# Batch 1's product of q and k-transposed-v in float32, with a newly derived list of steps

## The chip, the cores and the metric

The kernel runs on one core of a Trainium2 chip. The metric is device time in microseconds (us). PE is TensorE, DVE is VectorE, ACT is ScalarE, POOL is GpSimd, and SP is SyncE, whose queue issues all transfers of this kernel. Between the engines only semaphores order the work; within one engine instructions run in the order of the program.

## The reference

Batch 8, 8 heads, 576 tokens, 64 channels a head; all in float32.

```python
q_s = softmax(q, axis=-1)            # over a head's 64 channels
k_s = softmax(k, axis=2)             # over the 576 tokens
kv  = einsum('bhsd,bhse->bhde', k_s, v)
x   = einsum('bhsd,bhde->bhse', q_s, kv)      # heads side by side: (8, 576, 512)
gate_pre = sum over t of conv_w[t] * x shifted down by 4 - t tokens   # 5 taps, zeros ahead
gate = sigmoid(gate_pre)
val  = x @ w_val                     # 512 x 512
out  = (gate * val) @ w_out          # 512 x 512
```

## The kernel before

The eight batches run through one pipeline. For each batch b, kv is summed from k and v by head pairs, q is transposed (q_turn, then q_turned copies it out of PSUM), and `attend b p` makes block p (128 of the 512 channels, all 576 tokens) of x in PSUM. From there x_high and x_low split a block into two float32r parts, first and four taps make the gate (a tap is one DVE instruction, or a scaled copy on ACT and an addition on POOL), sigmoid closes it. `value b m` multiplies x by w_val in three float32r products (low weights by high x, high by high, high by low), gated multiplies val by the gate, g_high and g_low split the result, `project b n` multiplies by w_out in the same way, and store copies a block out and sends it to memory. Weights arrive as 64-bit words (load_words) and are turned to float32 and split by part, field, scaled, signed, joined, w_high and w_low in the first 60 us. k's maximum over the tokens comes for batches 0 and 1 from a copy laid out by channels (load_kc, k_top, k_raise, k_turn), for the others from blocks km (load_km, k_peak), which go by way of memory (k_row, k_spread) to all partitions (k_sub, k_exp).

`attend` has two forms. For a batch in F32_BATCHES, batch 0 alone before, the main 512 tokens are one float32 product of kvd and the transposed q (`qh`). For the others kv is split by kv_high and kv_low and q by the type of qT and q_low, and three float32r products are summed: low kv by high q, high by high, high by low. The last 64 tokens are a float32 product in both.

The order is a list written out by hand or program, ORDER, of some 900 steps in one sequence; each step issues its instructions on its engines, so each engine and SP's queue run their share of it in that order. A letter behind a step names the engine: a ACT, v DVE, p POOL; l and r are the left and right half of the tokens. `warm n` issues n transposes into a spare bank; `warm 0` issues none. PSUM has two banks for x, q's transposes and the like (tag "x") and two for products (tag "mm"). The words, kvs and qTlo tiles share four buffers; the parts f of the weights and the km blocks share three; q, k and v have two buffers each. A load whose buffer is in use stops SP's queue, and all loads and stores behind it.

## Time and profile before

| | |
|---|---|
| median of three runs | 322.0 us (321.49 to 322.12) |
| the profiled execution | 320.3 us, its span 318.5 us |
| busy: PE | 297.3 us (93%) |
| busy: DVE | 271.5 us (85%) |
| busy: ACT | 204.6 us (64%) |
| busy: POOL | 188.7 us (59%) |
| read from memory, written | 41.4 MB, 9.5 MB |

PE's ends are modelled and its instructions overlap, so a pace is read from the distance of starts, not from durations. The page's busy shares are means over stages; the chain of waits and the timeline show what a stage waits for. A duration on DVE or ACT has some 0.06 us of overlap with the next one's start.

### The profile page before, as it was taken

Reading aid. Unit: us, or ns where it says so; the run is one execution under the profiler, and the core shown is the slowest. Engines: PE = TensorE matmul, PEld = TensorE weight load, DVE = VectorE, ACT = ScalarE, POOL = GpSimd, SP = SyncE. Lnnn points to the kernel's source line nnn. Section 1 sums busy time; section 2 is a strip of 40 time slices with the busy share of each in tenths; the row PEclk is TensorE's granted clock in tenths of the full one; section 3 lists DMA queues with packets and bytes.
Section 4 is the critical chain, followed back from the end, with each engine's and each line's share of the span. In section 5 each row is a group of like instructions: output and inputs, shape, how many; then the busy total and the mean of one; then the engine's idle time right before and its main releaser. Section 6 shows DMA issues by size and latency. Waiting matters only on the chain.

```text
span 318.5 us, 6426 instructions
## 1 busy us (share of the span) xinstructions
PE 297.3 (93%) x2557; PEld 276.4 (87%) x2557; DVE 271.5 (85%) x374; ACT 204.6 (64%) x316; POOL 188.7 (59%) x157
## 2 busy tenths in 40 slices
...
GB/s 250 370 390 174 410 396 199 194 8 175 238 264 264 74 181 139 254 189 112 143 64 313 50 232 283 160 16 355 82 0 37 39 77 2 0 74 76 0 42 108
DMA packets 20525, 51.25 MB, mean 161 GB/s; under 512 B 2832, under 2 KB 7312, under 8 KB 17808
## 3 DMA queue, kind: packets, MB, share of 16 engines
...
q8 instruction: 20, 0.33, 0.4%
...
HBM read 41.39 MB, written 9.45 MB: 160 GB/s over the span
## 4 chain that ended last, share of the span: by engine, by line
PE 55%; DVE 19%; DMA 16%; issue 4%; ACT 4%; SPq 1%; DVEq 0%; ACTq 0%
PE out L542 22%; PE val L542 20%; DVE gate L524 5%; DMA km<-in_k_strided 5%; PE x L498 4%; PE kv L433 4%; DMA words<-in_w_out 3%; DMA out<-o 2%; DMA q<-in_q 2%; DMA q<-in_q_tail 2%; PE qTps L465 2%; DVE qm L347 2%; DVE g L563 2%; DVE qs L362 2%; DVE kpk L274 2%
## 5 line engine op out<-in xcount | busy, mean ns | idle before, releaser
L524 DVE SCALAR_TENSOR_TENSOR gate<-x,cw,gate 128x575 f32<-128x575 f32 (+3 forms) x99 | 78.0, 807 | 3.3 <-POOL gate L528 1.5
L528 POOL TENSOR_TENSOR gate<-gate,far 128x572 f32<-128x572 f32 (+3 forms) x29 | 39.5, 1363 | 39.2 <-ACT far L527 38.9
L542 PE MATMUL out<-gh,w_out_lo 128*128 128x288 f32 x256 | 57.0, 301 | 0.7 <-ACT gh L160 0.7
L542 PE MATMUL val<-xh,w_val_lo 128*128 128x288 f32 x256 | 56.5, 302 | 0.8 <-DVE o L162 0.7
L542 PE MATMUL out<-gl,w_out_hi 128*128 128x288 f32 x256 | 55.6, 296 | 0.9 <-DVE gl L571 0.9
L542 PE MATMUL val<-xl,w_val_hi 128*128 128x288 f32 x256 | 55.0, 296 | 0.9 <-DVE xl L518 0.9
L542 PE MATMUL out<-gh,w_out_hi 128*128 128x288 f32 x256 | 55.4, 295 | 0.0
L542 PE MATMUL val<-xh,w_val_hi 128*128 128x288 f32 x256 | 54.8, 295 | 0.0
L571 POOL TENSOR_TENSOR gl<-g,gh 128x576 fp32r<-128x576 f32 x25 | 36.8, 1476 | 29.5 <-ACT gh L160 23.1
L542 PEld LDWEIGHTS out<-gl,w_out_hi 128*128 128x128 f32 x256 | 41.4, 188 | 1.4 <-DVE gl L571 1.4
L542 PEld LDWEIGHTS val<-xh,w_val_lo 128*128 128x128 f32 x256 | 40.9, 188 | 1.8 <-DVE o L162 0.9
L542 PEld LDWEIGHTS val<-xl,w_val_hi 128*128 128x128 f32 x256 | 41.2, 188 | 1.2 <-DVE xl L518 1.2
L542 PEld LDWEIGHTS out<-gh,w_out_lo 128*128 128x128 f32 x256 | 41.2, 189 | 1.0 <-ACT gh L160 1.0
L542 PEld LDWEIGHTS out<-gh,w_out_hi 128*128 128x128 f32 x256 | 41.5, 188 | 0.0
L542 PEld LDWEIGHTS val<-xh,w_val_hi 128*128 128x128 f32 x256 | 41.3, 188 | 0.0
L389 POOL TENSOR_TENSOR q<-q,qs 128x512 f32<-128x512 f32 x25 | 26.2, 1070 | 14.7 <-DVE qs L364 14.7
L563 DVE TENSOR_TENSOR g<-val,gate 128x576 f32<-128x576 f32 x32 | 23.9, 749 | 9.9 <-PE val L542 7.3
L527 ACT ACTIVATE far<-x,cw 128x572 f32<-128x572 f32 (+3 forms) x29 | 21.0, 737 | 14.2 <-DVE gate L524 9.3
L160 ACT CAST gh<-g 128x576 fp32r<-128x576 f32 x25 | 16.7, 672 | 17.5 <-DVE g L563 17.4
L160 ACT COPY o<-out 128x576 f32<-128x576 f32 (+1 forms) x22 | 13.5, 618 | 22.1 <-PE out L542 12.1
L531 ACT ACTIVATE gate<-gate 128x576 f32<-128x576 f32 x32 | 21.6, 685 | 6.1 <-DVE gate L524 3.5
L289 POOL TENSOR_TENSOR k<-k,kmax 128x512 f32<-128x512 f32 x18 | 24.9, 1397 | 0.9 <-DMA kmax<-krow 0.9
...
## 6 DMA issues: line engine op xcount, KB each, us to landing
out<-o SPq DMA_DIRECT2D x31, 288.0 KB, 2.3
v<-in_v SPq DMA_DIRECT2D x8, 1040.0 KB, 7.7
...
km<-in_k_strided SPq DMA_DIRECT2D x24, 288.0 KB, 3.2
...
kc<-in_k_channels SPq DMA_DIRECT2D x8, 288.0 KB, 8.1
...
```

The costliest lines, as they stand in the source:

```text
L160: nc.scalar.copy(out=out, in_=in_)
L289: engine(e).tensor_sub(kk[r, cs], kk[r, cs], mx[r, cs])
L389: engine(e).tensor_mul(qq, qq, s.unsqueeze(2).broadcast_to([P, H, D]))
L433: nc.tensor.matmul(acc[h * D:(h + 1) * D, p, :], T["k", b][:, c, cs] if c < 4 else ktz[b % 2][:, cs], T["v", b][:, c, hd] if c < 4 else T[ ...
L498: nc.tensor.matmul(ps[:, :MAIN], a, z, start=(i == 0), stop=(i == len(parts) - 1))
L524: nc.vector.scalar_tensor_tensor(out=a, in0=x, scalar=w, in1=a, op0=ALU.mult, op1=ALU.add)
L527: nc.scalar.activation(part, x, AF.Copy, scale=w)
L528: nc.gpsimd.tensor_add(a, a, part)
L531: nc.scalar.activation(T["gate", b, p], T["gate", b, p], AF.Sigmoid)
L542: nc.tensor.matmul(ps[:, cs], a[:, kb, ms], z[kb][:, cs], start=(kb == 0 and i == 0), stop=(kb == NB - 1 and i == 2),)
L563: nc.vector.tensor_mul(T["g", b, m], T["val", b, m], T["gate", b, m])
L571: engine(e).tensor_sub(T["gl", b, m], T["g", b, m], T["gh", b, m].bitcast(F32))
```

## The change

Batch 1 joins F32_BATCHES: its four x products are single float32 products, its qT is float32, and the steps kv_high 1, kv_low 1, q_low 1 0 and q_low 1 1 leave the list. The list is written anew: 902 steps in place of 906, nearly all of them moved against others, one of the two `warm 8` gone. No function is changed. Over the list 15 taps move from DVE to ACT and POOL, 12 g_low from POOL to DVE, three stores from DVE to ACT, three q_sub from DVE to POOL, two q_mul from DVE to ACT. The loads have another order; near the start q's first piece leads, k 2 stands where q 2 stood, and q 2 and k 3 come later. The last product is project 7 0 whole; before it was the left half of project 7 3.

```diff
-F32_BATCHES = (0,)
+F32_BATCHES = (0, 1)
...
-    load_kc 0 1, load_q 0 0 2, load_words 8, k_top 0 1, load_ident, q_lift 0 0, q_max 0 0 2, q_peak 0 0 2,
-    load_kc 0 0, k_top 0 0, load_words 1, load_kc 0 3, load_q 0 2 5, field 1, q_top 0 0 2 v, field 8, load_words 3,
...
-    k_top 0 2, load_kc 1 2, k_top 1 1, load_v 0, load_kc 1 3, w_high 1 a, load_kc 1 0, scaled 3 v, q_peak 0 2 5,
...
-    q_mul 0 2 v, kv 0, scaled 0 a, q_mul 0 1 p, q_mul 0 3 p, k_top 1 0, warm 8, q_turn 0 0, field 2, kv_norm 0 v,
...
-    q_mul 0 4 p, joined 0 p, part 2 a, tail_turn 0, load_q 2, tail_turned 0 a, load_k 3, signed 2, attend 0 1,
...
-    sigmoid 0 3, q_low 1 0, attend 1 0, q_turned 1 1 a, g_high 0 2 a, q_sub 2 0 p, g_high 0 1 a, load_kt 2, q_low 1 1,
...
-    load_km 3 3, attend 1 2, k_sub 2 3 p, first 1 2 a, k_sub 2 4 p, project 0 3, store 0 2 a, k_sub 2 1 p,
...
-    g_high 7 3 v, g_low 7 3 v, g_low 7 2 p, project 7 2, project 7 1, store 7 2 v, store 7 1 a, project 7 3 r,
-    project 7 0, store 7 3 a r, store 7 0 v, project 7 3 l, store 7 3 a l,
+    load_q 0 0 2, load_words 8, load_ident, q_max 0 0 2, field 8, q_lift 0 0, part 8 a, load_kc 0 1, load_kc 0 0,
+    load_words 1, q_peak 0 0 2, load_kc 0 3, load_q 0 2 5, q_top 0 0 2 a, k_top 0 1, load_words 3, load_kc 1 2,
...
+    joined 3 p, q_sum 0, k_tail_turn 0, q_exps 1 0 p, q_exps 1 3 p, k_top 1 0, k_top 1 3, k_turn 0 1, load_v 0,
+    k_top 1 1, k_tail_turned 0 a, q_exps 1 2 p, q_mul 0 2 v, q_mul 0 3 p, q_mul 0 1 p, joined 8 p, q_mul 0 4 v,
+    k_turned 0 1 a, scaled 0 a, k_raise 1 3, q_mul 0 0 a, kv 0, q_turn 0 0, w_high 3 a, tail_turn 0, k_raise 1 0,
+    signed 0, load_words 2, field 2, q_turned 0 0 a, kv_norm 0 v, k_raise 1 1, joined 0 p, q_turn 0 1,
+    tail_turned 0 a, scaled 2 p, q_sum 1, attend 0 1, load_words 5, field 5, load_words 4, part 2 v, load_k 2,
+    signed 2, load_v 1, q_turned 0 1 a, first 0 1 a, load_words 7, x_high 0 1 a, tap 0 1 3 v, w_low 3 p, w_high 0 a,
...
+    first 0 2 a, load_q 2, kv_norm 1 a, tap 0 3 2 v, load_k 3, x_low 0 3, load_kt 2, part 5 a, value 0 0, tap 0 2 3 v,
...
+    x_high 1 3 v, x_high 1 2 a, x_low 1 2, sigmoid 1 0, x_low 1 3, tap 1 2 3 v, value 1 0, first 1 3 v, tap 1 3 3 v,
+    warm 0, k_sub 2 1 p, load_km 4 1, load_q 3, q_exp 2, project 0 3, tap 1 2 2 v, warm 0, gated 1 0, tap 1 3 2 a,
...
+    load_km 5 2, first 2 0 a, x_high 2 1 a, store 1 0 a, k_sub 3 4 p, x_low 2 0, tap 2 0 3 v, load_k 4, k_sub 3 3 p,
...
+    g_high 7 2 a, value 7 3, gated 7 3, g_low 7 2 p, g_high 7 3 a, g_low 7 3 v, project 7 1, project 7 3 l,
+    store 7 1 a, project 7 3 r, project 7 2, store 7 3 a l, store 7 2 v, store 7 3 a r, project 7 0, store 7 0 a,
```

## Rows read from the trace of the kernel before

**Rows 1.** The chain of waits from 286 us on: start, length (us), work.

```profile
302.52 12.80 PE out L542 x96
```

**Rows 2.** PE's timeline: start, length (us), line, work, shape, count.

```profile
45.55 0.52 PE L542 MATMUL val<-xh,w_val_lo 128*128 128x288 f32 x2
87.69 0.51 PE L433 MATMUL kv<-v,k 128*64 128x65 f32 x10
```

**Rows 3.** PE's timeline: in brackets the idle time before, and its releaser.

```profile
82.31 0.54 PE L542 MATMUL val<-xl,w_val_hi 128*128 128x288 f32 x2 [0.93 <-DVE xl L518]
```

**Rows 4.** PE's groups from 87.7 us: busy us, mean ns, idle before.

```profile
L498 PE MATMUL x<-qT,kvs 128*128 128x512 f32 x48 | 16.1, 417 | 2.4 <-DVE qTlo L475 1.1 <-ACT far L527 1.1
L433 PE MATMUL kv<-v,k 128*64 128x65 f32 x384 | 14.6, 223 | 0.4 <-DVE o L162 0.4
```

**Rows 5.** PE's timeline around two kinds of x product.

```profile
32.74 1.08 PE L498 MATMUL x<-qT,kvd 128*128 128x512 f32 x2
33.65 0.33 PE L499 MATMUL x<-qTt,kvd 128*128 128x64 f32 x2
74.05 0.63 PE L498 MATMUL x<-qT,kvs 128*128 128x512 f32 x2
74.75 0.33 PE L499 MATMUL x<-qTt,kvd 128*128 128x64 f32 x2
```

**Rows 6.** Groups by line and form: busy us, mean ns, idle before.

```profile
L475 DVE TENSOR_TENSOR qTlo<-qTps,qT 128x1024 fp32r<-128x1024 f32 x14 | 16.7, 1214 | 0.5 <-ACT qT L160 0.5
L524 DVE SCALAR_TENSOR_TENSOR gate<-x,cw,gate 128x573 f32<-128x573 f32 x27 | 21.7, 808 | 1.8 <-POOL gate L528 1.4
L528 POOL TENSOR_TENSOR gate<-gate,far 128x572 f32<-128x572 f32 x11 | 15.9, 1447 | 5.3 <-ACT far L527 5.1
L160 ACT COPY o<-out 128x576 f32<-128x576 f32 x20 | 12.7, 639 | 16.8 <-issue 9.0 <-PE out L542 6.8 <-DMA out<-o 0.9
```

**Rows 7.** DVE's timeline: q's reduction, then three x_low.

```profile
11.96 1.75 DVE L347 TENSOR_REDUCE qm<-q 128x24 f32<-128x1536 f32 x1 [0.16 <-DMA q<-in_q_tail]
47.74 0.75 DVE L518 TENSOR_TENSOR xl<-x,xh 128x576 fp32r<-128x576 f32 x1
81.51 1.41 DVE L518 TENSOR_TENSOR xl<-x,xh 128x576 fp32r<-128x576 f32 x2
```

**Rows 8.** ACT's timeline: q_raise 0 2 and the first gate of batch 0.

```profile
20.90 0.60 ACT L420 ACTIVATE q<-qlps 128x512 f32<-128x512 f32 x1 [0.31 <-PE qlps L416]
33.00 0.72 ACT L512 ACTIVATE gate<-x,cw 128x576 f32<-128x576 f32 x1
```

**Rows 9.** Sums of waits: us in total, times, longest; SP's queue, then DVE.

```profile
SPq L196 <- PE qTtps L481: 9.2, 1, 9.2
DVE kpk L274 <- DMA km<-in_k_strided: 4.1, 4, 1.8
```

**Rows 10.** Instructions on gl: duration ns least/median/most.

```profile
L571 POOL TENSOR_TENSOR gl<-g,gh x25: 1422/1430/1938, 55.8 to 301.0; 128x576 fp32r<-128x576 f32 x25
L571 DVE TENSOR_TENSOR gl<-g,gh x7: 745/757/1683, 61.1 to 304.0; 128x576 fp32r<-128x576 f32 x7
```

**Rows 11.** Issues of transfers: count, KB each, median us to landing.

```profile
v<-in_v SPq DMA_DIRECT2D x8, 1040.0 KB, 7.7
out<-o SPq DMA_DIRECT2D x31, 288.0 KB, 2.3
out<-o SPq DMA_DIRECT2D x2, 144.0 KB, 1.7
```

**Rows 12.** ACT's timeline at the end.

```profile
315.34 0.40 ACT L160 COPY o<-out 128x288 f32<-128x288 f32 x1 [4.35 <-PE out L542]
```

**Rows 13.** One stretch: busy us by engine, granted clock, DMA share, GB/s.

```profile
13.00:14.00 1.00, 0.77 (x4) 0.34 (x4) 1.00 (x3) 0.74 (x2) 0.27 (x2) 0.50 1.13 459
```

**Rows 14.** PE's timeline: k_turn 0 0 and k_turn 0 1.

```profile
11.84 1.79 PE L319 MATMUL kps<-ident,kc 128*128 128x128 f32 x8
21.26 1.04 PE L319 MATMUL kps<-ident,kc 128*128 128x128 f32 x8
```

More of the change, by code (lines that the diff above doesn't have):

```diff
@@ L43 @@
-    q_turn 0 1, load_words 4, field 4, q_turned 0 0 a, signed 0, q_turned 0 1 a, scaled 2 a, q_sum 1, w_high 3 v,
-    q_mul 0 4 p, joined 0 p, part 2 a, tail_turn 0, load_q 2, tail_turned 0 a, load_k 3, signed 2, attend 0 1,
-    k_raise 1 2, first 0 1 a, x_high 0 1 a, load_v 1, field 5, tap 0 1 3 v, tap 0 1 2 v, tap 0 1 1 v, k_raise 1 0,
-    joined 2 p, k_raise 1 3, attend 0 0, k_tail_turn 1, w_low 3 p, warm 8, first 0 0 a, x_low 0 1, x_high 0 0 a,
-    tap 0 1 0 v, k_turn 1 0, w_high 0 a, k_tail_turned 1 a, tap 0 0 3 v, q_mul 1 3 p, x_low 0 0, scaled 5 a,
@@ L68 @@
-    g_high 1 1 a, tap 1 3 0 v, g_low 1 1 v, sigmoid 1 2, value 1 2, gated 1 2, load_km 4 0, warm 0, tail_turn 2,
-    kv_high 2 a, q_turn 2 0, k_sub 3 0 v, k_peak 4 0, tail_turned 2 a, sigmoid 1 3, q_turn 2 1, load_v 3,
-    q_turned 2 0 a, g_low 1 0 p, g_high 1 2 a, q_turned 2 1 a, q_low 2 0, k_sub 3 4 p, load_q 3, kv_low 2 p,
-    g_low 1 2 p, value 1 3, attend 2 1, q_low 2 1, attend 2 0, x_high 2 1 a, gated 1 3, q_max 3, first 2 1 a,
-    g_high 1 3 a, first 2 0 a, k_sub 3 1 p, load_km 4 2, tap 2 0 3 v, x_low 2 1, tap 2 0 2 v, g_low 1 3 p,
@@ L93 @@
-    q_turn 4 0, k_sub 5 3 p, tap 3 3 0 v, q_sub 5 2 p, q_turn 4 1, kv_norm 4 v, kv_high 4 v, value 3 2,
-    q_turned 4 0 a, tail_turned 4 a, kv_low 4 p, value 3 3, q_sub 5 3 p, q_turned 4 1 a, g_low 3 0 p, k_peak 6 1,
-    sigmoid 3 3, q_low 4 0, gated 3 2, q_low 4 1, attend 4 0, gated 3 3, first 4 0 a, attend 4 1, load_km 7 3,
-    g_high 3 2 v, load_q 6, x_high 4 0 a, g_high 3 3 v, g_low 3 2 p, first 4 1 v, q_exp 5, load_k 6, g_low 3 3 p,
-    tap 4 1 3 a, tap 4 0 3 v, x_low 4 0, project 3 2, tap 4 1 2 a, tap 4 0 2 v, x_high 4 1 a, project 3 1,
```

168 lines of the change are left out of this document (88 added, 80 removed).

## Prediction

> **What bounds the kernel now.** The page's busy shares come first: PE is the busiest engine and DVE the second, and neither share says which of them sets the end. So I went on to the chain of waits and to PE's timeline. From 286 us the chain is PE alone: the last four out products take 12.80 us, 3.20 us a product [rows 1]. Before the first val product at 45.55 us PE runs in pieces: nearly each step there waits for a transfer, DVE or ACT. Between 45.55 and the third kv product at 87.69 us [rows 2] it stops for DVE's results, longest for the low part of an x block, 0.93 us [rows 3]. After 87.69 us it idles 2.4 us ahead of the x products and 0.4 us ahead of kv, and hardly anywhere else [rows 4]. So three stages have three limits: DVE (with ACT and DMA) up to 46 us, DVE against PE up to 88 us, PE after that. Each is costed by itself.
>
> **Part 1: batch 1's x products (attend 1).** An x product in three float32r parts goes from 74.05 to 74.75 us in its main piece, 0.70 us; one in float32 from 32.74 to 33.65 us, 0.91 us [rows 5]. Four of them: 4 x 0.21 = +0.84 us of PE work. Removed are two q_low on DVE, 1.21 us each [rows 6], so 2.42 us, and kv_high on ACT and kv_low on POOL, for which nobody waited. Where the two q_low stood, 58 to 63 us, DVE works without a pause, and PE waits for DVE afterwards [rows 3]; so DVE's 2.42 us count, and PE's 0.84 us are covered as long as PE still waits there for more than that. Were DVE no limit, the part would cost 0.84 us.
> The Trainium skill (FP8 and Floating Point Precision, TensorE Precision Notes) counts four passes for true float32, against three single passes here: by it the ratio would be 4/3, an estimate of 0.93 us from 0.70, and the sum would be 0.1 us larger; the row is used.
>
> **Part 2: the list up to the first val product.** New and old load the same bytes ahead of q's second piece (kc 0 1, 0 0 and 0 3, q's first piece, words 8 and 1, ident), so DVE's reduction of that piece, which starts at 11.96 us when q's tail has landed [rows 7], is taken as unmoved. From its end to the last x_low of batch 0 DVE had 39 steps, 35.2 us by the mean durations of their groups, and took 34.8 us (13.71 to 48.49 us, first and last of them in [rows 7]): no gaps. The new list has 38 steps, 34.3 us there: four taps, scaled 3 and w_high 3 go, two other taps, q_mul 0 4, part 2 and field 7 come. That is -0.9 us. Against it stands ACT. From the end of q_raise 0 2 (21.50 us) to the first gate of batch 0 (33.00 us) [rows 8] ACT had 13.0 us of steps in 11.5 us, since instructions overlap at their ends; the new list puts k_raise 1 3, 1 0, 1 1 and w_high 3 ahead of that gate, 14.3 us, so 12.7 us at the same overlap. q_raise 0 2 itself ends some 0.9 us sooner, since the new list has less PE work before it, so the gate comes at 33.3 us in place of 33.0. Walking DVE on from there by hand (each step after the last, each tap after its gate), x_low 0 3 ends at 48.3 us against 48.49. I take 0; the bounds are -0.9 us (DVE's sum alone) and +3 us (ACT's steps without overlap, and half the clock, rival A). SP's queue improves: SP stood 9.2 us at load_q 2, with all later loads behind it [rows 9]; in the new list k 2 and v 1 go there, whose buffers are free, and q 2 stands behind v 2 and km 2 1.
>
> **Part 3: from the first val product to kv 2.** From x_low 0 3 to x_low 1 3 DVE had 38 steps and 32.3 us, and took 34.4 us (48.49 to 82.92, [rows 7]): 2.1 us of pauses, mostly for km transfers, for which DVE waits 4.1 us in all [rows 9]. The new list has 36 steps and 29.9 us: 2.42 us less for q_low, the rest exchanges. The km loads are queued earlier, so I keep 0.6 us of the pauses: x_low 1 3 ends at 48.3 + 29.9 + 0.6 = 78.8 us. value 1 0 can end 0.7 us later. New is that project 0 3 (3.2 us) follows it in place of leading it; then comes value 1 1 (3.2 us): kv 2 starts at 78.8 + 0.7 + 6.4 = 85.9 us in place of 87.69. That is -1.7 us, with PE's 0.84 us of part 1 inside. Bounds: -0.3 (all pauses stay) and -2.4 us (none). ACT's work from x_low 0 3 to the last q_turned of batch 2 grows from 37.1 to 39.8 us in some 47 us, so it has room, though not much.
>
> **Part 4: from kv 2 to the last val products.** Fifteen more taps go from DVE (0.81 us each) to ACT with an addition on POOL (1.45 us) [rows 6], and twelve g_low go from POOL (1.43 us) to DVE (0.76 us at the median) [rows 10]. Over the whole list DVE has 13.8 us less, ACT 18 us more (two more table loads among it), POOL 10 us more. PE's steps are the same but for their order, so only PE's 2.8 us of idle [rows 4] can be regained, or new idle be made. DVE's results for batch 2's val products come 4.7 us of its work earlier. I take -1.0 us, with bounds -2.8 and +3: load_v 3 now stands behind k 4 and a store, about 10.6 us of PE work before kv 3, and v's landing takes 7.7 us [rows 11] without a megabyte of k ahead of it.
> What speaks against the change in this part: DVE's seven g_low lasted 745 ns at least, 757 at the median and 1683 at most [rows 10], so one at least was held. The Trainium skill (SBUF — State Buffer, Who interferes with whom) says that a DVE instruction with two SBUF inputs and a GpSimd one that reads SBUF contend, and that the one that comes second waits for the other to end; the row agrees with it in some of the seven, and by that rule at its worst the time is that of rival B.
>
> **Part 5: the end.** The old list ends with half an out product: a copy of 0.40 us and a transfer of 144 KB, 1.7 us [rows 11, 12]. The new list ends with a whole tile: 0.64 us for ACT's copy [rows 6] and 288 KB, 2.3 us [rows 11]. +0.24 + 0.6 = +0.84 us; nothing covers it, and this is the surest term.
>
> **Sum.** 0 - 1.7 - 1.0 + 0.8 = -1.9 us. The profiled execution took 320.3 us, its span 318.5 us; so 318.4 us for one like it. The median of the three runs is 322.0 us, 1.7 us above; taken from that, 320.1 us.
>
> **Rivals.**
> A, no change: the gain is lost at the start. In the new list kv 0 waits for v 0, which is loaded behind three kc, and for k_tail_turned, by ACT's walk until 24.8 us. PE's step before it ends at about 21.1 us, so PE would stand 3.6 us, and the eight warming transposes behind kv 0 are gone. After the pauses around 9 us PE's granted clock was 0.50 (1.2 GHz) at 13 us [rows 13], and k_turn 0 0 took 1.79 us where k_turn 0 1 took 1.04 at 2.4 GHz [rows 14]. At half the clock kv 0 and the turns cost some 2 us more on the way to batch 0's first x, and value 0 0 is 1.9 us late: 322.0 us. For it: ACT and PE have no slack between 21 and 33 us. Against it: DVE has other work to do until 35 us.
> B, slower: DVE and POOL hold each other. Nineteen g_low on DVE, more additions on POOL: if each of the twelve moved took 1.68 us in place of 0.76, DVE gets 11 us back of its 13.8. Then parts 3 and 4 regain nothing, part 1's 0.84 us and part 5's 0.84 us stand, and one more wait of the size of 0.93 us [rows 3] comes in the middle: 322.0 + 0.8 + 0.8 + 0.9 = 324.5 us. It decides once the mean g_low on DVE passes about 1.3 us. Against it: the median of the row.
> C, faster still: DVE's relief removes all of PE's 2.8 us after kv 2, and the start gains its 0.9 us: 322.0 - 0.9 - 2.4 - 2.8 + 0.8 = 316.7 us.
> That the change doesn't do what it says: batch 1's x products would still read a qTlo at 60 us, with DVE's 2.4 us, and the time would be 322 us. I give it next to nothing, since the tuple F32_BATCHES alone decides it.
>
> **Chances.** The forecast, 318.4 to 321.3 us, 0.45; C and what lies toward it 0.15; A, 321.4 to 322.6 us, 0.17; B and any other slower case 0.23. A difference under 0.2% (0.64 us) can't be told from no change here. Faster 0.60, same 0.17, slower 0.23. The range takes in C to the edge and B with some 0.7 us of a late v 3: 316.5 to 325.2 us.
>
> **What would show it.** Part 1: four x products of batch 1 at 0.91 us in the main piece, and no qTlo before batch 2. Part 2: value 0 0 starts between 45 and 46.5 us; at 47.5 or later it is A, and PE's clock between 22 and 30 us tells which half of it. Part 3: kv 2 at about 86 us. Part 4: PE's idle after kv 2 below 2.8 us; kv 3 waiting for v would be the load order, long g_low on DVE would be B. Part 5: 0.84 us more from the last product to the end. The prediction is wrong if PE idles more than before in the middle, which sums per engine can't exclude: they say that no engine is full, not that no step comes late.

## The result and the profile after

The changed kernel takes 323.7 us (median of 20 executions, 321.2 to 326.2) against 321.5 us for the kernel before (20 executions, 318.3 to 326.5): 1.0092 times as long, 95% interval 1.0065 to 1.0119. The ratio, here and in the table below, leaves out executions more than 1.5% above the fastest of their kernel (three of the 20 here, three of e15's 12, two of e17's 6); the two medians, which leave out none, differ by 0.7%. The changed kernel is slower by 0.9%. The forecast was 320.1 us and faster.

The profiled execution of the changed kernel took 324.0 us, its span 322.1 us, 3.6 us more than before. Line numbers are one lower than in the kernel before. First the page: PE's busy time with its share and count, the granted clock in 40 slices, and the group of the taps on DVE (busy us, mean ns, idle before).

```profile
PE 299.2 (93%) x2545; PEld 278.7 (87%) x2545; DVE 265.9 (83%) x358; ACT 222.4 (69%) x350; POOL 198.9 (62%) x166
...
PEclk9797999989999999999979999999999999999999
...
L523 DVE SCALAR_TENSOR_TENSOR gate<-x,cw,gate 128x575 f32<-128x575 f32 (+3 forms) x84 | 66.9, 807 | 0.8
```

DVE was busy 265.9 us in place of 271.5. The forecast sum of moved steps was 13.8 us less; so some 8 us came back, as longer instructions; the places that matter are shown below. ACT has 222.4 us (18 more, as summed) and POOL 198.9 us (10 more, as summed). In the row of the clock the 7s and the 8 (at 8, 24, 64 and 161 us) are slices that hold a stretch at half speed.

PE's timeline (start, length in us, line, work, shapes, count, and in brackets the idle time before with its releaser) shows the places that matter, in order of time:

```profile
45.63 0.53 PE L541 MATMUL val<-xh,w_val_lo 128*128 128x288 f32 x2
...
61.31 1.08 PE L497 MATMUL x<-qT,kvd 128*128 128x512 f32 x2
62.22 0.33 PE L498 MATMUL x<-qTt,kvd 128*128 128x64 f32 x2
...
64.79 0.53 PE L541 MATMUL out<-gl,w_out_hi 128*128 128x288 f32 x2 [0.60 <-POOL gl L570]
...
68.85 0.54 PE L541 MATMUL out<-gl,w_out_hi 128*128 128x288 f32 x2 [2.20 <-DVE gl L570]
...
88.99 0.51 PE L432 MATMUL kv<-v,k 128*64 128x65 f32 x10
...
162.08 1.08 PE L432 MATMUL kv<-v,k 128*64 128x65 f32 x16 [3.44 <-ACT k L292]
```

Value 0 0 starts at 45.63 us, as before [rows 2]. An x product of batch 1 goes from 61.31 to 62.22 us in its main piece, 0.91 us, in float32, as forecast. Then project 0 1 stops twice for g_low, 0.60 and 2.20 us, where the longest stop of the stretch was 0.93 us [rows 3]. Kv 2 starts at 88.99 us, 1.3 us later than before and 3.1 us later than forecast. Kv 4 waits 3.44 us for k_exp.

PE's groups from 87.7 us (busy us, mean ns, idle time before and its releasers) answer to [rows 4]:

```profile
L432 PE MATMUL kv<-v,k 128*64 128x65 f32 x384 | 16.2, 236 | 4.0 <-ACT k L292 3.4 <-DMA v<-in_v 0.6
L497 PE MATMUL x<-qT,kvs 128*128 128x512 f32 x48 | 15.9, 412 | 0.0
```

The x products no longer wait at all (2.4 us before); kv waits 4.0 us (0.4 before), 3.4 of it ahead of kv 4. The 0.6 us for v are the late load_v 3. The last four out products stand as before [rows 1], in the chain of waits (start, length, work), but 3.2 us later:

```profile
305.69 12.79 PE out L541 x96
```

What PE does right after its two long pauses is read from the granted clock (busy us of PE, PEld, DVE, ACT, POOL with their counts, then PEclk, DMA share, GB/s):

```profile
69.00:70.00 1.00, 1.00 (x8) 1.00 (x9) 1.00 (x2) 0.57 (x1) 0.95 (x1) 1.00 0.00 0
70.00:73.00 3.00, 3.00 (x15) 3.00 (x14) 2.96 (x5) 1.87 (x4) 1.28 (x1) 0.50 0.69 228
161.00:162.00 1.00, 0.00 (x0) 0.00 (x0) 0.96 (x2) 1.00 (x2) 0.00 (x0) 1.00 0.08 2
162.00:165.00 3.00, 2.92 (x55) 2.92 (x57) 1.75 (x3) 2.98 (x6) 1.67 (x2) 0.53 0.24 55
```

A microsecond after the pause that ends at 68.85 us, and right behind the one that ends at 162.08 us, PE is granted 0.50 (1.2 GHz) for some 3 us. Its work is the same, so it takes longer: project 0 0 by 1.5 us, kv 4 by 1.6 us. The kernel before had no such stretch after 16 us. The Trainium skill (TensorE: Matmul & The Clock Gate, Part 1) says that the clock follows how busy PE has been; the trace agrees. But a pause of this size isn't always followed by half clock. In e3 and e10 below PE stops for the same 2.2 us in project 0 1, and in e2 and e5 for 3.2 us ahead of kv 4, and the clock stays at its full level; e2's first kv products there take 0.69 us where the changed kernel's took 1.08:

```profile
160.69 0.69 PE L433 MATMUL kv<-v,k 128*64 128x65 f32 x16 [3.19 <-ACT k L293]
```

Nor is slower work always lost: from the start of kv 4 to PE's end the kernels take 156.4, 156.2 and 156.1 us where half clock comes there (changed, e10, e14), and 156.2 us where it doesn't (e2, e5). So the 1.6 us at kv 4 are made up later, but for 0.2 us or less.

To compare executions, the time is cut at four points of PE: the start of value 0 0, kv 2, kv 4, and the end of the last product. The last column is from there to the end of the span. All in us, from each kernel's profile; "mended" is explained below.

| kernel | value 0 0 at | to kv 2 | to kv 4 | to PE's end | rest | ratio to before [95%] |
|---|---|---|---|---|---|---|
| before | 45.6 | 42.1 | 72.1 | 155.5 | 3.2 | |
| changed | 45.6 | 43.4 | 73.1 | 156.4 | 3.7 | 1.0092 [1.0065, 1.0119] |
| e1 old list, float32 | 47.6 | 40.1 | 75.8 | 155.2 | 3.2 | 1.0001 [0.9961, 1.0042] |
| e2 new list, three parts | 46.0 | 43.6 | 71.1 | 156.2 | 3.7 | 1.0177 [1.0123, 1.0231] |
| e3 k_sub on POOL | 49.5 | 41.9 | 69.4 | 156.2 | 3.7 | 1.0050 [1.0003, 1.0096] |
| e4 k_sub earlier | 48.4 | 43.4 | 70.1 | 156.0 | 3.7 | 1.0055 [1.0015, 1.0095] |
| e5 g_low first | 45.7 | 43.8 | 71.1 | 156.2 | 3.7 | 1.0125 [1.0063, 1.0188] |
| e6 both moves | 49.3 | 43.7 | 70.1 | 156.0 | 3.7 | 1.0032 [0.9991, 1.0074] |
| e7 both, warming at kv 0 | 48.0 | 42.2 | 70.0 | 156.0 | 3.7 | 1.0129 [1.0050, 1.0208] |
| e8 short train | 48.1 | 43.4 | 69.5 | 156.2 | 3.7 | (one execution, 322.6 us) |
| e9 before, 20 products first | 47.0 | 40.6 | 72.6 | 155.0 | 3.2 | 0.9998 [0.9960, 1.0036] |
| e10 changed, 20 products first | 44.7 | 41.8 | 72.2 | 156.2 | 3.7 | 1.0104 [1.0047, 1.0161] |
| e11 mended, both warmings | 46.1 | 40.8 | 72.5 | 156.1 | 3.2 | 1.0006 [0.9969, 1.0043] |
| e12 mended | 48.1 | 40.8 | 71.6 | 156.2 | 3.2 | 0.9980 [0.9949, 1.0011] |
| e13 mended, three parts | 46.3 | 42.8 | 72.4 | 156.1 | 3.2 | 1.0102 [1.0053, 1.0151] |
| e14 w_high on ACT | 45.0 | 42.9 | 73.0 | 156.1 | 3.7 | 1.0110 [1.0046, 1.0173] |
| e15 mended, k_sub earlier | 48.2 | 40.8 | 70.5 | 156.0 | 3.2 | 0.9974 [0.9931, 1.0017] |
| e16 e15, 12 products first | 46.1 | 40.8 | 71.2 | 156.1 | 3.2 | 0.9921 [0.9889, 0.9953] |
| e17 before, 12 products first | 47.2 | 41.3 | 72.8 | 155.3 | 3.3 | 0.9899 [0.9847, 0.9952] |

The change cost nothing up to value 0 0, 1.2 us up to kv 2, 1.0 us up to kv 4, 0.9 us behind it and 0.4 us at the end. Executions of one kernel spread over 3 to 8 us, and the first column is a part of that spread (see the start, below). Most of what follows is read from the stretches behind value 0 0, but these are of one execution each. The changed kernel and e10, with the same steps there, take some 273 and 270 us from value 0 0 to PE's end. And the profiled execution is often not a typical one: in e2, e5, e7 and e10 it is 2.4 to 4.2 us under the kernel's median, in e1, e6, e12 and e17 2.1 to 3.9 us above it.

### The profile page after: what moved, and what is told of

Read it like the earlier page. It is cut to its first block, busy times and chain, and to the rows that moved or that the text cites. A ratio compares the mean times of both kernels' runs of the same rounds, so it can differ in the third digit from the quotient of the medians.

```text
span 322.1 us, 6415 instructions
## 1 busy us (share of the span) xinstructions
PE 299.2 (93%) x2545; PEld 278.7 (87%) x2545; DVE 265.9 (83%) x358; ACT 222.4 (69%) x350; POOL 198.9 (62%) x166
## 4 chain that ended last, share of the span: by engine, by line
PE 56%; DVE 24%; DMA 9%; issue 4%; ACT 3%; SPq 1%; POOL 1%; DVEq 0%; POOLq 0%; ACTq 0%
PE out L541 23%; PE val L541 20%; DVE gate L523 5%; PE kv L432 5%; PE x L497 4%; DVE qs L361 3%; DMA v<-in_v 3%; DMA kc<-in_k_channels 3%; PE qTps L464 2%; DMA q<-in_q_tail 2%; DVE gl L570 2%; DVE k L288 2%; DVE g L562 2%; DVE xl L517 1%; DVE kpk L273 1%
## 5 line engine op out<-in xcount | busy, mean ns | idle before, releaser
L527 POOL TENSOR_TENSOR gate<-gate,far 128x572 f32<-128x572 f32 (+3 forms) x44 | 59.2, 1352 | 56.1 <-ACT far L526 55.2
L523 DVE SCALAR_TENSOR_TENSOR gate<-x,cw,gate 128x575 f32<-128x575 f32 (+3 forms) x84 | 66.9, 807 | 0.8
L541 PE MATMUL out<-gl,w_out_hi 128*128 128x288 f32 x256 | 56.4, 299 | 3.1 <-DVE gl L570 2.5
L541 PEld LDWEIGHTS out<-gl,w_out_hi 128*128 128x128 f32 x256 | 41.9, 190 | 4.1 <-DVE gl L570 3.2
L526 ACT ACTIVATE far<-x,cw 128x572 f32<-128x572 f32 (+3 forms) x44 | 31.7, 742 | 17.0 <-DVE gate L523 9.3
L541 PEld LDWEIGHTS out<-gh,w_out_hi 128*128 128x128 f32 x256 | 42.2, 191 | 0.0
L541 PEld LDWEIGHTS out<-gh,w_out_lo 128*128 128x128 f32 x256 | 41.8, 191 | 0.4 <-ACT gh L159 0.2
L541 PEld LDWEIGHTS val<-xh,w_val_hi 128*128 128x128 f32 x256 | 41.3, 188 | 0.0
L541 PEld LDWEIGHTS val<-xl,w_val_hi 128*128 128x128 f32 x256 | 41.3, 188 | 0.0
L159 ACT COPY o<-out 128x576 f32<-128x576 f32 (+1 forms) x25 | 15.2, 621 | 22.0 <-PE out L541 20.3
L432 PE MATMUL kv<-v,k 128*64 128x65 f32 x512 | 22.2, 239 | 7.3 <-ACT k L292 3.4
L350 POOL TENSOR_TENSOR q<-q,qm 128x512 f32<-128x512 f32 x25 | 27.0, 1098 | 1.6 <-PE val L541 0.9
L570 POOL TENSOR_TENSOR gl<-g,gh 128x576 fp32r<-128x576 f32 x13 | 19.4, 1495 | 13.2 <-ACT gh L159 9.6
```

Of the source, the lines that this page charges most:

```text
L159: nc.scalar.copy(out=out, in_=in_)
L350: engine(e).tensor_sub(qq, qq, T["qm", b][:, cs].unsqueeze(2).broadcast_to([P, H, D]))
L432: nc.tensor.matmul(acc[h * D:(h + 1) * D, p, :], T["k", b][:, c, cs] if c < 4 else ktz[b % 2][:, cs], T["v", b][:, c, hd] if c < 4 else T[ ...
L523: nc.vector.scalar_tensor_tensor(out=a, in0=x, scalar=w, in1=a, op0=ALU.mult, op1=ALU.add)
L526: nc.scalar.activation(part, x, AF.Copy, scale=w)
L527: nc.gpsimd.tensor_add(a, a, part)
```

## The experiments

The theory after the result: the list costs the time, not float32; in it DVE and POOL hold each other in two places, PE pauses there, and each pause is followed by a stretch at half clock. The rivals: float32 itself costs it; the pauses hide one another, so that mending them gives nothing; the time is lost at the start.

### Float32 or the list (e1, e2)

e1 is the old list with batch 1 in float32; e2 is the new list with batch 1 in three parts.

```diff
e1  -F32_BATCHES = (0,)
    +F32_BATCHES = (0, 1)
    -kv_high 1 a ... kv_low 1 p ... q_low 1 0 ... q_low 1 1
e2  -F32_BATCHES = (0, 1)
    +F32_BATCHES = (0,)
    +kv_high 1 a ... kv_low 1 p ... q_low 1 1 ... q_low 1 0
```

> The list of the kernel before, without kv_high 1, kv_low 1, q_low 1 0 and q_low 1 1, and with batch 1 in F32_BATCHES: part 1 of the change alone. Theory (the new list lost the time by holds of DVE beside POOL, and by PE's clock after the pauses that they make): part 1 is worth about what the prediction said, -1.6 to 0 us against the kernel before, and PE's granted clock stays at its full level after 50 us. Rival (float32 in batch 1 itself costs the time): +2 us or more, as the whole change did.

> The new list with batch 1 in three float32r parts, the four steps put back behind the steps that feed them (kv_high 1 and kv_low 1 behind kv_norm 1 and q_mul 1 0, each q_low behind its q_turned). Theory: slower than before, as the whole change is, by 2 to 6 us, as the loss comes from the list and DVE gets 2.4 us more around 58 us. Rival (float32 in batch 1): back at the time of the kernel before, within 0.5 us.

e1 can't be told from the kernel before; e2 is 1.8% slower. The list costs the time. Within the new list float32 pays: the changed kernel is 0.9% faster than e2, and the intervals don't meet. In the old list it brings nothing that can be seen. e1 does take 40.1 us from value 0 0 to kv 2 in place of 42.1, but its value 0 0 was 2.05 us late, and kv 2 starts at 87.69 us in both. DVE's timeline of the kernel before, then e1's, has the reason: ahead of the last two x_low it waits for the same block of km, which lands at the same time.

```profile
80.84 0.76 DVE L274 TENSOR_REDUCE kpk<-km 128x1 f32<-128x576 f32 x1 [1.09 <-DMA km<-in_k_strided]
```

```profile
80.84 0.75 DVE L273 TENSOR_REDUCE kpk<-km 128x1 f32<-128x576 f32 x1 [1.17 <-DMA km<-in_k_strided]
```

x_low 1 3 ends at 82.92 us in both. The old list in three parts shortens the stretch too when it starts late: 40.6 and 41.3 us from value 0 0 at 47.0 and 47.2 us (e9, e17). Behind kv 2 e1 lost time; DVE's timeline and PE's show where:

```profile
104.67 2.29 DVE L346 TENSOR_REDUCE qm<-q 128x32 f32<-128x2048 f32 x1 [3.34 <-DMA q<-in_q]
```

```profile
114.28 1.22 PE L497 MATMUL x<-qT,kvs 128*128 128x512 f32 x2 [2.77 <-ACT far L526]
```

Q 3 lands too late for q_max 3: DVE waits 3.34 us (1.7 us in the kernel before), the taps behind it come late, and PE stops 2.77 us ahead of an x product and then works at half clock. So what float32 freed on DVE in the old list ran into transfers; that is read from the trace and wasn't tried by moving the loads alone. The second place is less sure: e1's profiled execution took 323.9 us against a median of 320.0, so its 3.34 us may be more than the usual wait (2.45 and 2.56 us in e9 and e17). In the new list neither step waits for a transfer.

### K_sub 4 3 and POOL's train (e3, e4, e8)

In the changed kernel DVE's k_sub 4 3 took 5.64 us; alone it takes 0.68. DVE's timeline, then POOL's, then ACT's:

```profile
153.11 5.64 DVE L288 TENSOR_TENSOR k<-k,kmax 128x512 f32<-128x512 f32 x1
```

```profile
152.90 1.29 POOL L288 TENSOR_TENSOR k<-k,kmax 128x512 f32<-128x512 f32 x1
154.15 1.04 POOL L350 TENSOR_TENSOR q<-q,qm 128x512 f32<-128x512 f32 x1
155.16 4.49 POOL L388 TENSOR_TENSOR q<-q,qs 128x512 f32<-128x512 f32 x4
```

```profile
158.82 1.28 ACT L292 ACT_TABLE_LOAD   x1 [3.87 <-DVE k L288]
```

POOL works from 152.90 to 159.64 us without a gap: a k_sub, a q_sub, and four q_mul of 1.03, 1.03, 1.03 and 1.48 us. DVE's instruction starts during the first of these six and ends 0.59 us after the sixth has started, at 158.16 us. K_exp 4, and with it kv 4, waits for it. e3 gives the step to POOL; e4 leaves it on DVE, but ahead of q_sum 4; e8 leaves it in its place and takes the last three q_mul off POOL's train.

```diff
e3  -k_sub 4 3 v
    +k_sub 4 3 p
e4  +k_sub 4 3 v, q_sum 4, ...
    -k_sub 4 3 v
e8  -q_mul 4 1 p ... q_mul 4 4 p, q_mul 4 2 p, gated 3 1
    +gated 3 1, q_mul 4 1 v, q_mul 4 4 v, q_mul 4 2 v
```

> The changed kernel with one letter changed: k_sub 4 3 on POOL in place of DVE, where it lasted 5.64 us beside a train of POOL instructions. Theory (the long k_sub makes k_exp 4 and kv 4 late, and PE's clock falls in the pause): PE's pause ahead of kv 4, 3.4 us, and the 1.6 us that kv 4 takes longer both go or shrink under 1 us, so -3 to -5 us against the changed kernel, 1 to 2.5 us under the kernel before. Rival (DVE's step is long because it waits for kmax or k, and POOL's would be as long): no change.

> The changed kernel with k_sub 4 3 still on DVE but ahead of q_sum 4, about 6 us earlier, where POOL stands idle soon after. Theory (POOL's neighbours hold it): it lasts 0.7 to 1.8 us there, kv 4 has no pause above 1 us, and the time is 3 to 5 us under the changed kernel. Rival (the instruction is slow by its data or its transfers, which would be even later there): it lasts as long as before or longer.

> k_sub 4 3 stays where the changed kernel has it, on DVE, beside POOL's k_sub 4 1, q_sub 5 1 and q_mul 4 0; the three q_mul behind them (4 1, 4 4, 4 2) go from POOL to DVE, behind gated 3 1. Theory (a DVE subtraction with two inputs waits until POOL's unbroken train of instructions ends): k_sub 4 3 lasts about 3.2 us, to the end of q_mul 4 0, in place of 5.64. Rival 1 (it waits for the one POOL instruction that runs at its start): about 1.5 to 2 us. Rival 2 (the length has nothing to do with POOL's train, for instance memory traffic): 5 us or more again.

DVE's k_sub 4 3 in e8, and POOL's instructions beside it:

```profile
154.98 2.62 DVE L288 TENSOR_TENSOR k<-k,kmax 128x512 f32<-128x512 f32 x1
```

```profile
154.75 1.29 POOL L288 TENSOR_TENSOR k<-k,kmax 128x512 f32<-128x512 f32 x1
155.99 1.05 POOL L350 TENSOR_TENSOR q<-q,qm 128x512 f32<-128x512 f32 x1
157.00 1.50 POOL L388 TENSOR_TENSOR q<-q,qs 128x512 f32<-128x512 f32 x1
```

It lasts 2.62 us: with three instructions in POOL's train it again ends 0.59 us after the last of them has started. That lies between the first theory (3.2 us) and rival 1 (1.5 to 2): it waited for two whole POOL instructions, so for more than the one that ran at its start, but got in ahead of the third, where I had let it wait for the train's end. Rival 2 is out. In e4 the train is cut by the neighbours there, and k_sub takes 1.30 us:

```profile
149.19 1.30 DVE L288 TENSOR_TENSOR k<-k,kmax 128x512 f32<-128x512 f32 x1
```

```profile
148.52 1.42 POOL L527 TENSOR_TENSOR gate<-gate,far 128x572 f32<-128x572 f32 x1
149.90 1.49 POOL L350 TENSOR_TENSOR q<-q,qm 128x512 f32<-128x512 f32 x1
```

Again 0.59 us after the start of a POOL instruction (149.90), and that one takes 1.49 us where its like took 1.04: POOL is held in its turn. In all three (changed, e8, e4) the POOL instruction that k_sub came ahead of is the last one before POOL pauses. Kv 4 then comes 69.4 to 70.1 us after kv 2 in all three, in place of 73.1, and no half clock follows. Part of that gain lies ahead of the hold: from kv 2 to kv 3 these stretches differ by up to 1.5 us. From kv 3 to kv 4 the five kernels with the long k_sub (changed, e2, e5, e10, e14) take 43.3 to 43.9 us, e3, e4 and e8 40.8 to 41.7, so the hold is worth 2 to 3 us there. In the total e3 and e4 stand at 1.0050 and 1.0055 in place of 1.0092, but the intervals overlap. So the hold is shown as one cause by the stretch and not by the total, and some 0.5% is left.

### The stretch up to kv 2 (e5, e14, e6)

From 57 to 70 us POOL is busy nearly throughout (joined, q_sub, g_low, a tap's addition, w_low), and DVE's steps beside it last longer than alone. DVE's timeline; the first line is the like of 57.52 and 64.94 without a neighbour:

```profile
10.53 0.43 DVE L248 TENSOR_SCALAR e<-e 128x512 int32<-128x512 int32 x1 [0.36 <-POOL e L167]
...
57.52 1.27 DVE L248 TENSOR_SCALAR e<-e 128x512 int32<-128x512 int32 x1
...
60.05 1.82 DVE L570 TENSOR_TENSOR gl<-g,gh 128x576 fp32r<-128x576 f32 x1
...
63.78 1.24 DVE L161 CAST w_out_hi<-f 128x512 fp32r<-128x512 f32 x1
64.94 1.26 DVE L248 TENSOR_SCALAR e<-e 128x512 int32<-128x512 int32 x1
...
66.85 1.95 DVE L570 TENSOR_TENSOR gl<-g,gh 128x576 fp32r<-128x576 f32 x1
...
79.45 0.76 DVE L161 CAST xh<-x 128x576 fp32r<-128x576 f32 x1 [2.27 <-PE x L498]
80.13 1.41 DVE L517 TENSOR_TENSOR xl<-x,xh 128x576 fp32r<-128x576 f32 x2
```

Signed 6 and 7 take 1.27 and 1.26 us in place of 0.43, two g_low 1.82 and 1.95 in place of 0.74, w_high 6 1.24 us (DVE's copy of w_val took 0.36 in the kernel before). That is 4.8 us of holds; in the kernel before I find 2.0 us of them in this stretch, g_low's 1.68 us [rows 10] and one field of 1.51 us. The Trainium skill (SBUF — State Buffer, Who interferes with whom) counts these kinds among those that can meet GpSimd at a shared port: two-input instructions, casts and tensor_scalar; and k_peak, a reduction, which it says never does, took 0.70 to 0.76 us throughout. The last two lines show the price: DVE idles 2.27 us for PE's x product, which is late by PE's pause, and only then x_low 1 2 and 1 3 follow.

e5 puts g_low 0 3 ahead of two steps that nobody waited for; e14 gives one of these to ACT and leaves the order; e6 is e5 and e4 together.

```diff
e5  -w_high 6 v, signed 7, g_low 0 3 v
    +g_low 0 3 v, w_high 6 v, signed 7        (g_high 0 3 a ahead of first 1 0 a)
e14 -w_high 6 v
    +tap 1 0 3 a, w_high 6 a
```

> Two DVE steps (w_high 6, signed 7) move behind g_low 0 3, and ACT's g_high 0 3 ahead of first 1 0; nothing else of the changed kernel moves. Theory (the order on DVE ahead of project 0 1, with holds by POOL, makes the pause): g_low 0 3 ends near 65.5 us in place of 68.8, PE's 2.20 us at 68.85 go, the stretch at half clock behind it too, project 0 1 and project 0 0 lose under 1.5 us together in place of 5.0; kv 2 near 86 us in place of 89.0; the time 1.0 to 3 us below the changed kernel, ratio to before 1.000 to 1.006. Rival (PE's time there is covered, since DVE sets the x blocks of batch 1): project 0 1's pause goes, but value 1 0 waits as much more for x_low, kv 2 stays at 88 to 89 us, ratio 1.009. The pause at kv 4 (3.6 us and half the clock behind it) stays under both.

> The changed kernel with one edit: w_high 6 is copied by ACT, behind tap 1 0 3, in place of DVE, where it took 1.24 us just ahead of signed 7 and g_low 0 3. Theory (DVE's work and its holds between 58 and 70 us set kv 2): g_low 0 3 ends 1.0 to 1.3 us sooner, project 0 1 loses 2.2 to 2.5 us in place of 3.4, kv 2 comes 1 us sooner (42.3 us after value 0 0 in place of 43.4), ratio 1.005 to 1.008. Rival (POOL's train holds whatever stands on DVE then): the next steps last longer by as much, kv 2 as before, ratio 1.009.

> The move of w_high 6 and signed 7 behind g_low 0 3, and k_sub 4 3 ahead of q_sum 4, together. Theory (two pauses of PE, each with a stretch at half clock behind it, are what the list costs): both pauses go, no dip of the clock between 60 and 300 us, the ratio to before is 0.993 to 1.001. Rival (other pauses take their place, or the start and the end cost the rest): ratio 1.003 to 1.006, no better than the k_sub move alone at 1.0055.

In e5 project 0 1 lost 1.0 us in place of 3.4, but behind project 0 2 PE stood 2.35 us for a tap on DVE, ahead of the next x product, and kv 2 stood where it was (43.8 us). DVE's timeline of e5:

```profile
64.04 1.41 DVE L570 TENSOR_TENSOR gl<-g,gh 128x576 fp32r<-128x576 f32 x1
65.38 1.27 DVE L161 CAST w_out_hi<-f 128x512 fp32r<-128x512 f32 x1
66.56 1.67 DVE L248 TENSOR_SCALAR e<-e 128x512 int32<-128x512 int32 x1
68.27 1.66 DVE L249 SCALAR_TENSOR_TENSOR e<-words,e 128x512 int32<-128x512 int32 x1
```

G_low comes sooner (1.41 us), but now signed 7's two instructions take 1.67 and 1.66 us where they took 1.26 and 0.69. The hold belongs to the stretch, not to the step: whatever DVE does there meets POOL. So the rival was right for e5, and in e14 too: signed 7's second instruction went to 1.42 us, kv 2 came 0.5 us sooner, not 1. In e6 kv 2 stands as in e5 and kv 4 as in e4; its ratio, 1.0032, is the rival's, at its lower end. e5's own ratio, 1.0125, is no lower than the changed kernel's.

One more thing is read from the table without a new edit. The changed kernel, e3, e4, e8 and e10 have the same steps up to kv 2. With the half clock after project 0 1's pause the stretch is 43.4 us (changed, e4, e8), without it 41.9 and 41.8 (e3, e10). e6 and e7, alike from kv 0 on, differ in the same way behind the pause at the tap: 43.7 us with half clock, 42.2 without. The stretch at half clock costs 1.5 us by itself.

### The start (e7, e9, e10)

Profiles of one list differ at the start. PE's timeline, q_minus 0 0 in the changed kernel and in e12:

```profile
9.48 1.98 PE L415 MATMUL qlps<-minus,qtop 8*128 8x512 f32 x4 [0.45 <-ACT qtop L159]
```

```profile
9.71 3.78 PE L415 MATMUL qlps<-minus,qtop 8*128 8x512 f32 x4 [0.45 <-ACT qtop L159]
```

The same four products take 1.98 us at full clock and 3.78 at half; in the second case the record of the granted clock shows its first rise some 8 us later (17.7 in place of 8.6 us), and value 0 0 stands at 48.1 us. Of twelve profiles of the new list with nothing put ahead of it six are of this kind (e3, e4, e6, e8, e12, e15: value 0 0 at 48.1 to 49.5 us), and one of the two of the old list (e1, 47.6). e7 puts 22 transposes ahead of kv 0, where PE stood 3.28 us and had half clock afterwards; e9 and e10 put 20 products of a zeroed tile ahead of everything.

```diff
e7  (e6) k_turn 0 1, +warm 22
e9, e10  +warm_first 20, (the list)
+    def warm_first(n):
+        ps, z = bank("warm"), kvd[0][:, 0]
+        for i in range(n):
+            nc.tensor.matmul(ps[:, ...], z, z, start=True, stop=True)
```

> As the one with both moves, and 22 warming transposes between k_turn 0 1 and kv 0, where PE stood 3.28 us. Theory: PE's clock is full at kv 0 (pitch 2.5 us in place of 3.8), q_turned and the first x of batch 0 come 0.5 to 1 us sooner, but value 0 0 moves by less than 0.5 us, since DVE sets it: ratio the same within 0.2% as without. Rival (the start is where the rest is lost, rival A of the prediction): value 0 0 comes 1 to 2 us sooner and the ratio falls by 0.3 to 0.6%.

> The kernel before, with 20 products of a zeroed tile on PE ahead of everything (no transfer needed for them), so that PE is busy until ident lands near 5 us. Seen so far in the profiles: q_minus 0 0 takes 1.95 to 1.98 us in some executions and 3.75 to 3.78 us in others of either list, and value 0 0 starts at 45.6 or at 47.6 us in the old list. Theory (PE's clock rises at a chance moment after PE starts work, and the later moment costs 2 us in the old list): with PE busy from the start q_minus 0 0 takes about 2 us in every run, value 0 0 starts at 45.6 us or sooner, the spread of the times falls from 6 us to under 3 us, and the median falls by 0 to 1.5 us. Rival (the spread comes from transfers): no change of spread or median.

> The changed kernel with the same 20 products ahead of everything. Theory (the new list's start is no dearer than the old one when PE's clock is full from the start; what it costs lies behind 46 us): value 0 0 at 45.6 us or sooner, ratio to before 1.003 to 1.009, above that of the old list with the same start by 0.9%. Rival (the new list loses at the start, since a late rise of the clock costs it 2.8 to 3.9 us where it costs the old one 2.0): ratio to before under 1.002, the two lists with the warm start within 0.4% of one another.

e7 answers another question than it was made for. PE's timeline:

```profile
24.82 3.90 PE L590 MATMUL warm<-ident 128*128 128x128 f32 x22 [3.29 <-ACT ktz L159]
28.65 1.00 PE L432 MATMUL kv<-v,k 128*64 128x65 f32 x16
```

The transposes themselves waited for a bank that ACT had not yet emptied; kv 0 starts at 28.65 us, 4.0 us later, and value 0 0 at 47.95 us, 2.3 us later than in a start of the same kind (changed kernel). So the way from kv 0 to value 0 0 has some 1.7 us of slack. In the total e7 is no faster than e6 (1.0129 against 1.0032). In e9 and e10 q_minus took 1.95 and 1.98 us, but 20 products held PE until 8.4 and 7.5 us, past ident's landing, and neither median moved; nor did e9's spread shrink, 6.2 us against 6.4. That the two lists differ by 1% with the same start as without it speaks against the start as the cause of the 0.9%.

### The mended list (e12, e11, e13, e15)

e12 has four edits of the new list: g_low 0 3 first as in e5, w_high 6 on ACT, k_sub 4 3 on POOL, and the old list's end, with half a product last. e11 adds both warmings, e13 takes float32 away from e12, e15 has e4's k_sub in place of e3's.

```diff
e12 -w_high 6 v, signed 7, g_low 0 3 v
    +g_low 0 3 v, signed 7 ... tap 1 0 3 a, w_high 6 a
    -k_sub 4 3 v
    +k_sub 4 3 p
    -project 7 1, project 7 3 l, store 7 1 a, project 7 3 r, project 7 2, ... project 7 0, store 7 0 a
    +project 7 2, project 7 1, ... project 7 3 r, project 7 0, ... project 7 3 l, store 7 3 a l
e11 (e12) +warm_first 20 ... k_turn 0 1, +warm 22 x
e13 (e12) -F32_BATCHES = (0, 1) ... +F32_BATCHES = (0,), +kv_high 1 a, kv_low 1 p, q_low 1 0, q_low 1 1
e15 (e12) -k_sub 4 3 p ... +k_sub 4 3 v, q_sum 4
```

> As the one before but without the two warmings: g_low 0 3 ahead of signed 7, w_high 6 on ACT, k_sub 4 3 on POOL, the old list's end. Theory: behind value 0 0 the same times as with the warmings, 269 to 271 us to the end; value 0 0 at 45.6 or at 48 to 49.5 us by the moment at which PE's clock rises; ratio to before 0.992 to 1.000. If the start has nothing to do with it, the same ratio as with the warmings.

> The changed kernel with five mends: PE busy from the start; 22 transposes in a bank of the x kind between k_turn 0 1 and kv 0; g_low 0 3 ahead of signed 7 and w_high 6 on ACT in place of DVE; k_sub 4 3 on POOL; the end of the old list (half a product last). Theory: value 0 0 near 45.5, from there to kv 2 41 us (changed kernel 43.4, with a stretch at half clock), to kv 4 69.5 (73.1), to PE's end 156, the end 3.2 us: the span 315 to 316.5, ratio to before 0.983 to 0.993. Rival (every mended pause comes back as another): 0.997 to 1.003.

> The mended list (g_low 0 3 ahead of signed 7, w_high 6 on ACT, k_sub 4 3 on POOL, the old list's end) with batch 1's x products in three float32r parts again: kv_high 1, kv_low 1, q_low 1 0 and q_low 1 1 are back. Theory (part 1 of the prediction: two q_low are 2.42 us of DVE between 58 and 63 us, PE saves 0.84 us): from value 0 0 to kv 2 it takes 1.0 to 2.0 us more than the 40.8 us of the same list in float32, the time lies 0.3 to 0.6% above that list's ratio of 0.998. Rival (DVE is no limit there, float32 costs PE's 0.84 us): it takes 0.5 to 0.9 us less, ratio 0.995 to 0.998.

> The mended list with k_sub 4 3 on DVE ahead of q_sum 4 in place of POOL (g_low 0 3 ahead of signed 7, w_high 6 on ACT, the old list's end as there). Theory: the stretches add up, 40.8 us from value 0 0 to kv 2, 70.05 us to kv 4 (as in the three runs with this k_sub; 71.6 with it on POOL), 156.1 to PE's end, 3.2 to the end: 270.1 us behind value 0 0 against 273.0 in the kernel before; ratio 0.990 to 0.996. Rival (kv 4 is set by another chain once kv 2 comes sooner, as with k_sub on POOL): 71.5 us or more from kv 2 to kv 4, ratio 0.997 to 1.000.

With the four edits the 0.9% are gone: 0.9980 and 0.9974. Kv 2 comes 40.8 us after value 0 0 in all three with float32, and no half clock follows project 0 1 any more (e11 had none at all before its end). The two warmings of e11, forecast at 0.983 to 0.993, gave nothing that can be seen (1.0006). Back in three parts (e13) it is 42.8 us, and the whole is 1.0% slower than the kernel before. Part 1's DVE term is in the timelines of DVE and PE, in the place that the prediction gave it:

```profile
61.62 2.34 DVE L475 TENSOR_TENSOR qTlo<-qTps,qT 128x1024 fp32r<-128x1024 f32 x2
```

```profile
62.98 0.71 PE L498 MATMUL x<-qT,kvs 128*128 128x512 f32 x2 [1.86 <-DVE qTlo L475]
```

The two q_low take 2.34 us, PE stands 1.86 us for them and is at half clock behind that, and the stretch is 1.9 us longer. In the total e13 is 1.2% slower than e12, some 3.9 us, twice what this stretch shows and twice the 0.3 to 0.6% forecast; where the rest is wasn't found. e15's kv 4 comes 70.5 us after kv 2, as expected; e12's 71.6. In the total the two can't be told apart, and e15's 0.9974 is its rival's. How much each of the four edits gives isn't separated beyond e3, e5 and e14.

### Work for PE from the start on (e16, e17)

```diff
e16 (e15)    +warm_first 12
e17 (before) +warm_first 12
```

> The mended list with k_sub 4 3 on DVE ahead of q_sum 4, and 12 products of a zeroed tile on PE ahead of everything (the 20 of the earlier runs held PE until 7.4 to 8.5 us, past the landing of ident near 5 us). Theory (PE's clock rises 8 us later in some executions than in others, and that costs the new list 2.5 us or more at value 0 0): q_minus 0 0 takes about 2 us, value 0 0 starts at 44.5 to 46 us in place of 48.2, behind it the same 270.5 us, the ratio to before is 0.986 to 0.993. Rival (the moment of the rise is not what separates the executions of one kernel): ratio 0.996 to 1.000 as without.

> The kernel before with the same 12 products ahead of everything. Theory: value 0 0 at 44.5 to 46 us in every execution, ratio to before 0.994 to 0.999. Rival (as above): 1.000, with as wide a spread as before.

With 12 products e16 is 0.8% faster than the kernel before, 318.6 us against 321.4 us on its chip, and all its executions lie between 316.3 and 320.0 us. That it is 0.5% faster than e15 (0.9974) isn't clear of noise, as the intervals overlap. e17 stands at 0.9899, but two of its six executions, 321.6 and 322.1 us, are no faster than the median of the kernel before. PE's timeline of e16:

```profile
1.29 4.94 PE L596 MATMUL warm<-kvd 128*128 128x128 f32 x24 [1.29 <-POOL kvd L610]
6.07 1.88 PE L410 MATMUL qlps<-q,ident 128*128 128x512 f32 x4
8.62 1.98 PE L415 MATMUL qlps<-minus,qtop 8*128 8x512 f32 x4 [0.45 <-ACT qtop L159]
```

The products end at 6.07 us, 1 us after ident has landed, and q_minus 0 0 takes 1.98 us. But value 0 0 stands at 46.1 and 47.2 us in these two profiles (e17's is of the execution of 321.6 us), no sooner than in an execution whose clock rises early by itself; the gain may be that the late kind becomes rare, which single profiles can't show. That the mended list keeps nothing over the old one when both start this way (0.9921 against 0.9899, intervals overlapping) is as far as the runs go.

## Why the prediction was wrong, part by part

- **What bounds the kernel:** the three stages and their limits were read rightly. In the old list a km transfer that lands at 80.84 us is a further limit of the second stage (e1). DVE's 2.4 us move kv 2 by 1.9 us in the mended list (e13, with half clock) and by nothing that can be told apart in e1; PE bounds the rest.
- **Part 1** was right: 0.91 us a product, q_low gone, DVE's time counting in that stretch. In the new list float32 is worth 0.9% (changed against e2), in the mended one 1.2% (e12 against e13). Alone in the old list it brings nothing (e1), where transfers are the next limit: km at 80.84 us, and q 3 behind it.
- **Part 2** was right: value 0 0 at 45.63 us, kv 0 at 24.61 after 3.28 us of standing. Rival A's half clock at kv 0 came as described (0.50 from 25.7 to 29.1 us) and cost nothing that can be seen: some 1.7 us of slack cover it (e7), and e11, which has no half clock at all on the way, reaches value 0 0 at 46.1 us. What the prediction didn't see is the chance moment at which PE's clock first rises.
- **Part 3 is the first step that failed.** Kv 2 was to come 7.1 us after x_low 1 3, and did (81.54 to 88.99, 7.4 us). But x_low 1 3 ended at 81.54 and not at 78.8 us, although x_low 0 3 ended at 47.50 and not at 48.3:

```profile
46.75 0.75 DVE L517 TENSOR_TENSOR xl<-x,xh 128x576 fp32r<-128x576 f32 x1
```

So the stretch took 34.0 us where the forecast had 30.5. The sum for DVE, "29.9 us", took each step at its unheld duration, g_low at the median of [rows 10]. In the trace 4.8 us of holds stand there, and PE's pause behind them, with 1.5 us of half clock, came back to DVE as 2.27 us of waiting. Together that is more than the 3.5 us missing, because most durations overlap the next by 0.08 us, which the sum counts twice: 2.6 us over 38 instructions. The same overlap hid the holds of the kernel before: the "2.1 us of pauses" are 3.0 us of idling and 2.0 us of holds, less 2.9 us of overlap. With the order and one engine changed, the mended list reaches 40.8 us from value 0 0 to kv 2; the forecast was 40.4.
- **Part 4 is the second.** Forecast -1.0 us, measured +1.9 (73.1 and 156.4 against 72.1 and 155.5). Without k_sub's hold (e4) it is 70.05 + 155.98 in place of 72.14 + 155.47 us, so -1.6 us: most of what failed is one instruction, though these are single profiles and only 2 to 3 us of the difference lie where the hold does. It is the kind of step for which the prediction cited the port rule; it then priced the holds by g_low's median. V 3 cost 0.6 us.
- **Part 5** had the right sign: 3.67 in place of 3.23 us, +0.4 in place of +0.84. The copy was as forecast (0.64 against 0.40 us). The transfer's term was too large: from the copy's end to the end of the span it is 3.0 us in place of 2.8, so 0.2 and not 0.6. ACT's timeline:

```profile
318.50 0.64 ACT L159 COPY o<-out 128x576 f32<-128x576 f32 x1 [5.69 <-PE out L541]
```

- **Rival B** was what happened, in its mechanism (DVE and POOL hold each other) but by another way than its condition; that its time came out near (324.5 forecast, 323.7 measured) is luck, as it was summed from twelve g_low held by 0.9 us each. It was to decide "once the mean g_low on DVE passes about 1.3 us". The instructions on gl in the changed kernel (least, median, most in ns) against [rows 10]:

```profile
L570 DVE TENSOR_TENSOR gl<-g,gh x19: 743/751/1952, 60.0 to 307.3; 128x576 fp32r<-128x576 f32 x19
L570 POOL TENSOR_TENSOR gl<-g,gh x13: 1416/1432/1937, 57.1 to 304.5; 128x576 fp32r<-128x576 f32 x13
```

Their mean on DVE is 0.99 us, and the median never moved. Four of the 19 lasted 1.59 to 1.95 us; PE waited right behind one of them (66.85 us). That one and the 5.64 us of a step of another kind stand ahead of PE's two long pauses. A mean can't carry such a threshold. By the Trainium skill's rule (SBUF — State Buffer, Who interferes with whom) the one issued first goes first and the other waits for it; in the trace POOL's q_sub started at 154.15, a microsecond after DVE's k_sub, and it and three more went ahead of it. Where the two differ, the measurement decides: k_sub waited until the last instruction of POOL's train.

What stays open: what decides when DVE gets in. In e4, e8 and the changed kernel it came ahead of the last instruction before POOL paused, but the g_low at 100.11 us in the changed kernel (1.59 us) came between two POOL instructions that followed without a gap. Open as well: why the clock fell behind some pauses of PE and not behind others of the same length; why 20 products ahead of everything changed no median where 12 did; and the 0.5 to 0.9 us that every version of the new list loses between kv 4 and PE's end.
